# Loading the first weights in three transfers instead of four, and the sink rows of v partly copied on chip

## The chip, the cores and the metric

One core of one Trainium2 chip runs the kernel. The core has a matrix engine (PE; its weight loads are shown apart as PEld), a vector engine (DVE), an activation engine (ACT), a general engine (POOL) and a sequencer that only issues transfers and waits (SP). SP, ACT and POOL each issue DMA transfers, which the profile shows as queues: q1 is SP's, q10 ACT's and q0 POOL's. All queues share 16 DMA engines. The metric is the time of one execution on the device, in microseconds (us).

## The reference

Attention with a window and with sinks, followed by a gated two-layer network over all heads:

```python
batch, n_heads, seq, head_dim = 4, 8, 768, 64;  n_sink, window = 4, 128
scores = q @ k^T / sqrt(64)
keep = (key < 4) | ((0 <= query - key) & (query - key < 128))
a = softmax(where(keep, scores, -1e9))
x = (a @ v) with the heads side by side          # (3072, 512)
h = x @ w_in                                     # w_in  (512, 2048)
out = (h / (1 + exp(-beta * h))) @ w_out         # w_out (2048, 512), out (3072, 512)
```

All inputs and the output are float32 in device memory. The kernel computes in bfloat16 and sums in float32.

## The kernel before, in words

**Units and tiles.** Attention is cut into 32 units n: one batch, one pair of heads and one half (384 positions) of the sequence each. `place(n)` gives the batch (n // 8), the pair and the half. Four units make one token tile T of 384 tokens, and there are 8 token tiles. In the network a tile has 16 hidden blocks of 128 columns (the index i runs over all 128 of them, m = i mod 16 within the tile). A hidden block is four products of w_in with the tile's x (L814), a tanh on ACT (L822) and a gate on DVE (L835). Its contribution to the output is three products with w_out (L843), one for each 128 tokens.

**Attention.** For units 0 to 11, q and k come by SP into float32 staging (L522), are cast to bfloat16 by POOL (for q of the first four by DVE, L621), transposed on PE (L652, L634), and multiplied into scores (L700), on which ACT takes the exponential (L707). From unit 12 on, POOL's transfers cast on the way (`land`, L552) and a DMA transpose on SP turns them (L567). v is cast into `v_aug`: for the first units by POOL's engine from staging (`cast_v`, L532), later by casting transfers (`load_v`, L542; `land_v`, L561). The product with v (L770) also gives the softmax sums; DVE takes the reciprocal (`rden`, L779) and scales (L781).

**Sinks.** A unit of the second half also attends to the first four keys of its sequence. Their keys come through `k_rows` (L592) into `k_sink`. The four rows of v lie in `v_sink`: for head 0 of each pair in partitions 0 to 3 and for head 1 in partitions 32 to 35, for all 16 pairs of batch and heads. Before the change two POOL transfers (L596) of 64 rows of 64 elements each, one for each head, bring all of them from device memory. They are read by the product at L759, which opens the sums of a second-half unit; the first such unit is unit 4.

**Weights.** w_in comes in four transfers of four blocks each (`load_w_in(m, 4)`, L578) issued by POOL, 1 MB of float32 each, which are cast on the way to 512 KB; one row of such a transfer is 512 elements, 2 KB. w_out comes in eight transfers of two blocks (L583).

**The order.** The kernel first collects every operation as a node with what it reads and writes. A planner then walks through time with estimated durations and a model of the transfers' landings, and puts each engine's nodes in the order in which they could start; ties go to the earlier written. What comes out is a fixed order for each engine; on the chip each engine runs it in order and waits on semaphores. A changed landing in the planner's model can thus change the order of other work. While PE has nothing to do before the first hidden block, the planner puts in fill products of a tile of ones (L450); from the first hidden block on there are none.

**Around the change.** POOL's first instructions alternate casts and issues: the first w_in transfer after `cast_v(0)`, the sink keys, the second w_in transfer, `cast_v(2)`, the third (14.02 us), `cast_v(3)`, the fourth (15.57), then `k_sink` and the masks, the two sink transfers of v (20.92), three loads of v, and the transfers of w_out with casts of q and k of units 4 to 7 in between. SP's loads of q and k of units 4 to 7 wait for the second w_in transfer to land; those of units 8 to 11 each wait for one of the w_out transfers. The later transfers of w_out wait for the third w_in transfer (block 8). The loop over s writes one step for each hidden block of the rest; s is not a time, but a place in the written order.

Of the kernel before, what the change touches and what calls it, by code (L numbers as in the profile page):

```python
# [9 lines left out]
B, H, S, D = 4, 8, 768, 64  # L10
NSINK, WINDOW = 4, 128
# [14 lines left out]
HEAD1 = 32  # L26
# [29 lines left out]
AGENDA = {}  # L56
for n in range(4, 8):
    for step, at in (("in", n - 4), ("sink", 16), ("a", 16), ("b", 16), ("av", 17), ("out", 18)):
        AGENDA.setdefault(at if step == "in" else at + 1 * (n - 4), []).append((n, step))
# [297 lines left out]
def bass_streamingllm_window__then__act_swish_beta_kernel(  # L357
# [218 lines left out]
    def load_w_in(m, ms, after=()):  # L576
        here = slice(m * 128, (m + ms) * 128)
        op("gp", lambda e: e.dma_start(w_in16[:, :, here], w_in_src[:, :, here]), after=after,  # L578
           w=[("w_in", c, mm) for c in range(4) for mm in range(m, m + ms)],
           dma=f"wi{m}", late=0.0 if m else 800.0, **transfer(DM * ms * 128 * 4, 385, 740.0, 3.0))  # L580
# [3 lines left out]
           w=[("w_out", mm) for mm in range(m, m + ms)],  # L584
           dma=f"wo{m}", **transfer(ms * 128 * NOUT * 4, 416, 740.0, 3.0))

    def load_sinks(x, after=()):
        for hh in range(2):
            rows = slice(HEAD1 * hh, HEAD1 * hh + NSINK)
            if x:  # L590
                src = k[:, :, 0:NSINK, :].rearrange("b (g h) s d -> h (b g) s d", h=2)[hh]
                op("gp", lambda e, hh=hh, src=src: e.dma_start(k_rows[:, :, hh, :], src),  # L592
                   w=[("k_rows", hh)], after=after, dma=f"sk{hh}", busy=650.0, lag=300.0, weight=0.4)
            else:
                src = v[:, :, 0:NSINK, :].rearrange("b (g h) s d -> s h (b g) d", h=2)[:, hh]
                op("gp", lambda e, rows=rows, hh=hh, src=src: e.dma_start(v_sink[rows, :, hh, 0:D], src),  # L596
                   w=[("v_sink", hh)], r=["v_sink"], after=after, dma=f"sv{hh}", busy=650.0, lag=400.0, weight=0.4)

    def sink_keys():

# [144 lines left out]
    def attend(n, av_ps=av_ps, name="av"):  # L745
        _, hp, half, pb = place(n)
        z = n % NE
        where = {}
        x = 0
        for runs in RUNS[half]:  # L750
            for kb, qb, nq in runs:
                for y in range(nq):
                    where[kb, qb + y] = x
                    x += 1
        with P.together("pe"):
            for mm in range(3):
                m, at = 3 * half + mm, mm * 2 * D1
                if half == 1:
                    op("pe", lambda e, at=at, mm=mm: e.matmul(  # L759
                        av_ps[:, at:at + 2 * D1], E_sink[z][:, mm * 128:mm * 128 + 128],  # L760
                        v_sink[:, n // 8 * 4 + hp, :, :].rearrange("p h e -> p (h e)"),
                        start=True, stop=False, skip_group_check=True),
                       r=[("E_sink", z), "v_sink", ("v_sink", 0), ("v_sink", 1)], w=[name],
                       **pe(130))
                for hh in range(2):
                    kbs = range(m + 1) if half == 0 else (m - 1, m)
                    for x, kb in enumerate(kbs):
                        col = 128 * where[kb, m]
# [107 lines left out]
    load_w_in(0, 4, [("v", 0, 0, 0)])  # L876
    cast_v(1)
    cast(2)
    load_sinks(1, [("v", 1, 0, 0)])
# [15 lines left out]
    cast(3)  # L895
    load_w_in(4, 4, [("k16", 0)])
    cast_v(2)
    load_w_in(8, 4, [("v", 2, 0, 0)])
    cast_v(3)
    load_w_in(12, 4, [("v", 3, 0, 0)])  # L900
    for n in range(4):
        if n < 2:
            transpose_first(n + 2)
        if n < 3:
            first_scores(n + 1)
        if n == 2:
# [31 lines left out]
    for s in range(-2, S_END + NM):  # L938
# [102 lines left out]
```

## Time and profile before

| what | value |
|---|---|
| median of 3 runs | 228.73 us (228.01 to 229.79) |
| profiled execution | 228.59 us |
| its span, first to last instruction | 226.9 us |
| granted PE clock, mean | 1.000 |
| first hidden product | 17.32 us |
| first product with w_out | 35.08 us |
| first hidden product of the second token tile | 44.51 us |
| POOL issues | w_in 0.74 to 0.94 us, v_sink 0.65, load of v 0.90, land 0.76 |

The span is what the timeline covers; the profiled execution's own time is 1.7 us longer. In the timeline a row merges neighbouring instructions of the same kind: start, length, engine, line, operation, result and operands, count, and in brackets the engine's idle time before it with what ended it. The length of a row of products includes the time that the last one takes to come through the array, so that the next row may start before this one has ended. In the list of transfers, the time to landing is from the issue to the last semaphore update.

### The profile page before, as it was taken

Reading aid. Unit: us, or ns where it says so; the run is one execution under the profiler, and the core shown is the slowest. Engines: PE = TensorE matmul, PEld = TensorE weight load, DVE = VectorE, ACT = ScalarE, POOL = GpSimd, SP = SyncE. Lnnn points to the kernel's source line nnn. Section 1 sums busy time; section 2 is a strip of 40 time slices with the busy share of each in tenths; the row PEclk is TensorE's granted clock in tenths of the full one; section 3 lists DMA queues with packets and bytes.
Section 4 is the critical chain, followed back from the end, with each engine's and each line's share of the span. In section 5 each row is a group of like instructions: output and inputs, shape, how many; then the busy total and the mean of one; then the engine's idle time right before and its main releaser. Section 6 shows DMA issues by size and latency. Waiting matters only on the chain.

```text
span 226.9 us, 4463 instructions
## 1 busy us (share of the span) xinstructions
PE 220.0 (97%) x1761; PEld 122.1 (54%) x1761; DVE 132.6 (58%) x264; ACT 141.3 (62%) x224; POOL 125.7 (55%) x191
## 2 busy tenths in 40 slices
PE   7999989999999999999999999999999999999995
PEld 4665545555555555555555555555555555555454
DVE  5466777488975776566565656555656564443200
ACT  1877796197586877566657766666656755555311
POOL 4689992899994979695939396876300000000000
PEclk9999999999999999999999999999999999999999
DMA  6999999999998999999999999998921012110122
GB/s 172 251 172 179 276 194 205 257 228 139 118 138 124 124 117 151 120 167 144 116 113 135 99 138 147 96 165 119 94 80 53 20 57 64 49 46 0 58 83 92
DMA packets 96901, 28.92 MB, mean 127 GB/s; under 512 B 83424, under 2 KB 93936, under 8 KB 96880
## 3 DMA queue, kind: packets, MB, share of 16 engines
q0 software_dynamic: 59232, 10.92, 65.7%
q1 hardware_dynamic: 34304, 16.79, 34.3%
q10 hardware_dynamic: 3344, 0.93, 1.9%
q8 instruction: 14, 0.23, 0.5%
q14 instruction: 7, 0.06, 0.1%
HBM read 27.34 MB, written 6.29 MB: 148 GB/s over the span
## 4 chain that ended last, share of the span: by engine, by line
PE 73%; DMA 15%; POOL 8%; issue 2%; SPq 1%; ACT 0%; POOLq 0%; ACTq 0%
PE acc L843 32%; PE h_ps L814 29%; DMA k_stage<-in_k_dram 8%; DMA w_out<-in_moe_w_out_dram 4%; PE s_ps L727 4%; PE s_ps L770 4%; POOL qk L621 3%; DMA w_in<-in_moe_w_in_dram 2%; POOL land L552 2%; PE h_ps L843 2%; POOL v_aug L561 1%; PE s_ps L759 1%; PE s_ps L670 1%; SPq L522 1%; POOL v_aug L532 0%
## 5 line engine op out<-in xcount | busy, mean ns | idle before, releaser
L822 ACT ACTIVATE th<-h_ps,beta_half 128x384 f32<-128x384 f32 x120 | 69.4, 581 | 59.7 <-PE h_ps L814 59.1
L843 PE MATMUL acc<-w_out,g 128*128 128x512 bf16 x368 | 99.7, 380 | 0.0
L814 PE MATMUL h_ps<-xT,w_in 128*128 128x384 bf16 x480 | 96.2, 326 | 0.0
L835 DVE SCALAR_TENSOR_TENSOR g<-th,h_ps 128x384 bf16<-128x384 f32 x120 | 65.6, 550 | 44.8 <-ACT th L822 44.0
L814 PEld LDWEIGHTS h_ps<-xT,w_in 128*128 128x128 bf16 x480 | 45.6, 98 | 39.8 <-issue 0.8
L843 PEld LDWEIGHTS acc<-w_out,g 128*128 128x128 bf16 x368 | 32.8, 98 | 28.8 <-issue 3.6
L552 POOL DMA_DIRECT2D land<-in_q_dram x40 | 30.2, 760 | 24.0 <-DVE rden L779 24.0
L552 POOL DMA_DIRECT2D land<-in_k_dram x40 | 30.3, 761 | 0.0
L561 POOL DMA_DIRECT2D v_aug<-in_v_dram x40 | 30.2, 760 | 0.0
L735 ACT ACTIVATE E<-s_ps 128x1536 bf16<-128x1536 f32 x20 | 28.8, 1442 | 0.0
L741 DVE TENSOR_TENSOR E<-E,mask 128x1536 bf16<-128x1536 bf16 x20 | 19.2, 958 | 16.4 <-ACT E L735 16.4
L851 ACT ACTIVATE out_sb<-acc 128x512 f32<-128x512 f32 x23 | 13.7, 596 | 7.6 <-PE acc L843 7.4
L770 PEld LDWEIGHTS s_ps<-v_aug,E 128*128 128x128 bf16 x336 | 15.2, 97 | 3.2 <-issue 1.2
L770 PE MATMUL s_ps<-v_aug,E 128*128 128x65 bf16 x336 | 16.8, 193 | 0.0
L707 ACT ACTIVATE E<-s_ps 128x768 bf16<-128x768 f32 x17 | 13.7, 811 | 4.3 <-PE s_ps L700 4.2
L781 DVE TENSOR_TENSOR o_norm<-s_ps,rden 128x384 bf16<-128x384 f32 x28 | 15.6, 556 | 0.8
L714 DVE TENSOR_TENSOR E<-E,mask 128x768 bf16<-128x768 bf16 x16 | 9.0, 572 | 2.0 <-ACT E L707 1.3
L727 PE MATMUL s_ps<-qkT 64*128 64x256 bf16 (+2 forms) x144 | 10.1, 254 | 0.0
L759 PE MATMUL s_ps<-v_sink,E_sink 128*128 128x130 bf16 x48 | 9.3, 219 | 0.0
L621 POOL CAST qk<-k_stage 128x384 bf16<-128x384 f32 x12 | 6.5, 544 | 4.7 <-DMA k_stage<-in_k_dram 4.4
L673 ACT ACTIVATE E_sink<-s_ps 128x384 bf16<-128x384 f32 x16 | 7.8, 490 | 1.5 <-PE s_ps L670 1.5
L727 PEld LDWEIGHTS s_ps<-qkT 64*128 64x128 bf16 x144 | 4.9, 94 | 7.1 <-issue 5.8
(75 smaller groups left out, 155.2 us busy)
## 6 DMA issues: line engine op xcount, KB each, us to landing
out_dram<-out_sb SPq DMA_DIRECT2D x23, 256.0 KB, 2.7
q_stage<-in_q_dram SPq DMA_DIRECT2D x12, 192.0 KB, 7.4
k_stage<-in_k_dram SPq DMA_DIRECT2D x12, 192.0 KB, 7.9
w_in<-in_moe_w_in_dram POOLq DMA_DIRECT2D x4, 512.0 KB, 6.8
w_out<-in_moe_w_out_dram POOLq DMA_DIRECT2D x8, 256.0 KB, 9.6
land<-in_q_dram POOLq DMA_DIRECT2D x40, 48.0 KB, 3.7
land<-in_k_dram POOLq DMA_DIRECT2D x40, 48.0 KB, 4.0
v_aug<-in_v_dram POOLq DMA_DIRECT2D x40, 48.0 KB, 3.4
```

What stands on the lines that cost most here:

```text
L552: op("gp", lambda e, d=d, s=s: e.dma_start(d, s), w=[("land", pb, half, x, hh)], after=after, dma=f"l{pb}{half}{x}{hh}", **transfer(TT * D ...
L561: op("gp", lambda e, d=d, s=s: e.dma_start(d, s), w=[("v", pb, 3 * half + c, hh) for c in range(3)], after=after, dma=f"lv{pb}{half}{hh}", ...
L707: op("act", lambda e: e.activation(both, src[:, :, 0:TT], AF.Exp, bias=0.0, scale=SCALE), x=list(names), w=[("E", n % NE, c)], **act(768))
L727: op("pe", lambda e, at=at, w=w, kb=kb, qb=qb, nq=nq, hh=hh, rows=rows, bank=bank: e.matmul(s_ps[:, 2 * hh + bank, at:at + w], keys_of(pb, ...
L735: op("act", lambda e: e.activation(E[z][:, :, :], src, AF.Exp, bias=0.0, scale=SCALE), x=list(S_NAMES), w=[("E", z, 0), ("E", z, 1)], **ac ...
L741: op("dve", lambda e: e.tensor_tensor(E[z][:, :, :], E[z][:, :, :], m.unsqueeze(1).to_broadcast([128, 2, 768]), ALU.mult), r=[("E", z, 0), ...
L770: last=(x == len(kbs) - 1): e.matmul(av_ps[:, at + hh * D1:at + hh * D1 + D1], E[z][:, hh, col:col + 128], v_aug[:, pb, hh, kb, 0:D1], sta ...
L781: op("dve", lambda e: e.tensor_tensor(o_norm[o][:, :, :, :].rearrange("p m h d -> p (m h) d"), src[:, :, 0:D], rden[z][:, :].unsqueeze(2). ...
L814: op("pe", lambda e: e.matmul(bank, w_in16[:, c, m * 128:(m + 1) * 128], xT[:, c, T * TT:(T + 1) * TT], start=(c == 0), stop=(c == 3)), r= ...
L822: op("act", lambda e: e.activation(th[i % 3][:, :], bank, AF.Tanh, bias=0.0, scale=beta_half[:, m:m + 1]), x=[name], r=["beta"], w=[("th", ...
L835: op("dve", lambda e: e.scalar_tensor_tensor(g[T % 2][:, m, :], th[i % 3][:, :], 1.0, bank, ALU.add, ALU.mult), r=[("th", i % 3)], x=[name ...
L843: op("pe", lambda e: e.matmul(bank[:, 0:width], g[T % 2][:, m, t * 128:(t + 1) * 128], w_out16[:, m, cols], start=(m == 0), stop=(m == NM ...
```

## The change

- The third and the fourth transfer of w_in become one: `load_w_in(8, 8)` brings blocks 8 to 15, 2 MB of float32 in rows of 4 KB, where the third was issued. The fourth issue goes.
- The two early transfers of v's sink rows go. For batch 0, DVE copies them from `v_aug` (rows 0 to 3 of the first key block, which the casts have just written), one copy for each head, written where the transfers were. For batch 1, DVE copies them likewise, written at step 34 behind a reciprocal.
- For batches 2 and 3 two transfers each bring them, written at steps 48 and 80. The product at L759 now waits for its own batch's rows.
- `load_sinks` is split: the sink keys are loaded as before. `1 * (n - 4)` becomes `n - 4`, which is the same.

```diff
-    def load_sinks(x, after=()):
+    def load_sink_keys(after=()):
+        for hh in range(2):
+            src = k[:, :, 0:NSINK, :].rearrange("b (g h) s d -> h (b g) s d", h=2)[hh]
+            op("gp", lambda e, hh=hh, src=src: e.dma_start(k_rows[:, :, hh, :], src),
+               w=[("k_rows", hh)], after=after, dma=f"sk{hh}", busy=650.0, lag=300.0, weight=0.4)
+
+    def sink_values(b, eng, after=()):
         for hh in range(2):
             rows = slice(HEAD1 * hh, HEAD1 * hh + NSINK)
...
-                src = v[:, :, 0:NSINK, :].rearrange("b (g h) s d -> s h (b g) d", h=2)[:, hh]
-                op("gp", lambda e, rows=rows, hh=hh, src=src: e.dma_start(v_sink[rows, :, hh, 0:D], src),
-                   w=[("v_sink", hh)], r=["v_sink"], after=after, dma=f"sv{hh}", busy=650.0, lag=400.0, weight=0.4)
+            op(eng, lambda e, rows=rows, hh=hh: e.tensor_copy(
+                v_sink[rows, 4 * b:4 * b + 4, hh, 0:D], v_aug[0:NSINK, :, hh, 0, 0:D]),
+               r=["v_sink", *(("v", z, 0, hh) for z in range(4))], w=[("v_sink", b, hh)],
+               busy=200.0, lag=140.0, after=after)
+
+    def load_sink_values(b):
+        for hh in range(2):
+            rows = slice(HEAD1 * hh, HEAD1 * hh + NSINK)
+            src = v[b, :, 0:NSINK, :].rearrange("(g h) s d -> s h g d", h=2)[:, hh]
+            op("gp", lambda e, rows=rows, hh=hh, src=src: e.dma_start(
+                v_sink[rows, 4 * b:4 * b + 4, hh, 0:D], src),
+               w=[("v_sink", b, hh)], r=["v_sink"], after=[("rden", 0)], dma=f"sv{b}{hh}", busy=650.0, lag=400.0, weight=0.4)
...
-                       r=[("E_sink", z), "v_sink", ("v_sink", 0), ("v_sink", 1)], w=[name],
+                       r=[("E_sink", z), "v_sink", ("v_sink", n // 8, 0), ("v_sink", n // 8, 1)], w=[name],
...
-    load_w_in(8, 4, [("v", 2, 0, 0)])
+    load_w_in(8, 8, [("v", 2, 0, 0)])
     cast_v(3)
-    load_w_in(12, 4, [("v", 3, 0, 0)])
...
-            load_sinks(0, [("v", 3, 0, 0)])
+            sink_values(0, "dve")
...
+        if s == 34:
+            sink_values(1, "dve", [("rden", 1)])
+        if s in (48, 80):
+            load_sink_values(2 if s == 48 else 3)
```

More of the change, by code (lines that the diff above doesn't have):

```diff
@@ L58 @@
     for step, at in (("in", n - 4), ("sink", 16), ("a", 16), ("b", 16), ("av", 17), ("out", 18)):
-        AGENDA.setdefault(at if step == "in" else at + 1 * (n - 4), []).append((n, step))
+        AGENDA.setdefault(at if step == "in" else at + n - 4, []).append((n, step))
 for n in range(8, NU):
@@ L585, in load_w_out @@
            dma=f"wo{m}", **transfer(ms * 128 * NOUT * 4, 416, 740.0, 3.0))
-    def load_sinks(x, after=()):
+    def load_sink_keys(after=()):
[4 more added lines that the diff above has]
+    def sink_values(b, eng, after=()):
         for hh in range(2):
             rows = slice(HEAD1 * hh, HEAD1 * hh + NSINK)
[L590 to L594, printed above, removed]
-                src = v[:, :, 0:NSINK, :].rearrange("b (g h) s d -> s h (b g) d", h=2)[:, hh]
-                op("gp", lambda e, rows=rows, hh=hh, src=src: e.dma_start(v_sink[rows, :, hh, 0:D], src),
-                   w=[("v_sink", hh)], r=["v_sink"], after=after, dma=f"sv{hh}", busy=650.0, lag=400.0, weight=0.4)
+            op(eng, lambda e, rows=rows, hh=hh: e.tensor_copy(
[9 more added lines that the diff above has]
+               w=[("v_sink", b, hh)], r=["v_sink"], after=[("rden", 0)], dma=f"sv{b}{hh}", busy=650.0, lag=400.0, weight=0.4)
     def sink_keys():
@@ L878, in bass_streamingllm_window__then__act_swish_beta_kernel @@
     cast(2)
-    load_sinks(1, [("v", 1, 0, 0)])
+    load_sink_keys([("v", 1, 0, 0)])
     select(ident32[:, :], ones32[:, :], [[1, 32]], ALU.is_equal, 0.0, 0, -1, ["ones32"], ["ident32"])
```

## The prediction

> **What bounds the kernel now.** I read the page's first part, then the chain of waits, then the timeline of PE stretch by stretch, then the DMA queues in narrow windows.
>
> The page's first part, and the longer pieces of the chain before 62 us (start, length, what):
>
> ```profile
> PE 220.0 (97%) x1761; PEld 122.1 (54%) x1761; DVE 132.6 (58%) x264; ACT 141.3 (62%) x224; POOL 125.7 (55%) x191
> ...
> 12.45 5.50 DMA w_in<-in_moe_w_in_dram
> 18.37 7.79 DMA k_stage<-in_k_dram
> ...
> 27.81 9.58 DMA w_out<-in_moe_w_out_dram
> 37.82 7.45 DMA k_stage<-in_k_dram
> ...
> 58.58 0.53 POOL qk L621
> ```
>
> After 59 us the chain is PE alone, one product behind the other to the end. So only what lies before 62 us can move the time. There the chain goes from transfer to transfer, and PE waits in small pieces. Its timeline (start, length, what, idle time before):
>
> ```profile
> 21.91 1.46 PE L814 MATMUL acc<-xT,w_in 128*128 128x384 bf16 x8
> 23.21 1.46 PE L814 MATMUL h_ps<-xT,w_in 128*128 128x384 bf16 x8
> 24.51 1.76 PE L814 MATMUL acc<-xT,w_in 128*128 128x384 bf16 x8
> 26.15 0.34 PE L634 MATMUL s_ps<-ident,qk 128*128 128x128 bf16 x3
> 26.78 0.34 PE L634 MATMUL s_ps<-ident,qk 128*128 128x128 bf16 x3 [0.29 <-POOL qk L621]
> ...
> 30.49 0.60 PE L634 MATMUL s_ps<-ident,qk 128*128 128x128 bf16 x6 [0.42 <-ACT qkT L641]
> ...
> 31.58 0.34 PE L700 MATMUL h_ps<-qkT 64*128 64x128 bf16 x4 [0.22 <-ACT E L707]
> ...
> 34.81 0.34 PE L700 MATMUL h_ps<-qkT 64*128 64x128 bf16 x4 [0.36 <-ACT E L707]
> ...
> 59.16 0.34 PE L634 MATMUL s_ps<-ident,qk 128*128 128x128 bf16 x3 [0.47 <-POOL qk L621]
> ```
>
> Eight hidden products start 1.30 us apart (21.91, 23.21, 24.51), so one takes 0.1625 us, and a block of four 0.65. The shown length contains a drain, so real idle is larger than the bracket: between starts, less issue slots, I get 0.34 before 26.15, 0.46 before 26.78, 0.8 around 30, about 1.9 from 31 to 35, and 0.35 at 50.2 and 0.64 at 58.5, where PE waits for POOL's casts. That is some 4.5 us in all which a better start could remove at most.
>
> The DMA queues: first 25 to 27 us, then 29 to 31, then 36 to 38 (packets, MB written, share). q0 is POOL's queue, q1 is SP's.
>
> ```profile
> q1 hardware_dynamic: 784, 0.57, 94.8%
> q0 software_dynamic: 499, 0.02, 23.6%
> ...
> q0 software_dynamic: 2059, 0.27, 205.1%
> q1 hardware_dynamic: 113, 0.08, 16.5%
> ...
> q0 software_dynamic: 427, 0.41, 124.2%
> ```
>
> From 25 to 27 us POOL's queue moves 0.02 MB: exactly the two sink transfers (8 KB each), and nothing behind them. SP's loads of q and k have the engines meanwhile.
>
> **The change, part by part.**
>
> *The third and fourth MB of w_in in one transfer.* Issues and landings before, from the windows around each issue: third 14.02 + 7.9 = 21.9, fourth 15.57 + 9.8 = 25.4. Hidden block 8, the first that reads them, comes at 21.91 + 0.65 = 22.56: just behind the landing. Now blocks 8 to 15 all wait for the whole 2 MB. When does it land? It is issued where the third was. Late bound: 25.4, the same bytes behind the same queue, with the same eight loads of SP (released by the second MB, at 17.96) beside them. Early bound: the queue alone moves a w_out MB in 2.5 us (four landings 1.28 us apart), so 17.94 + 2 x 2.5 = 23.0. The case nearest to it is the fourth MB itself; with half the packets I take 25.2. PE then stands still for 25.2 - 22.56 = 2.6 us (0.5 to 2.9). Nothing else is ready for it: the fill products end with the first hidden block, and the next transposes need casts of loads that land at 25.2 and 26.2.
>
> The Trainium skill, DMA: Bandwidth & Descriptors, Anatomy of one DMA, has a fixed 2.0 us for each such transfer beside bytes / 436 GB/s; by that one issue of 2 MB in place of two would land about 2 us earlier and the stall would be some 0.6 us. The 1.28 us between landings of queued 512 KB transfers shows no fixed part, so here I don't count it.
>
> What of the 2.6 us comes back: blocks 8 to 15 now run 25.2 to 30.4 and, with 12 transposes of 0.055, to about 31. That work lies where PE idled before (0.34 + 0.46 + 0.8 = 1.6 us). PE is 1.0 us late at 31 (range -1.1 to +1.3). ACT gets its tanh later too (eight of 0.615 us after 25.2); it then has a solid chain of exponentials, 29.65 to 36.2 before.
>
> *One POOL issue less (0.74 us and 0.3 of wait), and the two sink loads less (1.29 us).* POOL comes 2.3 us earlier to the loads of v and w_out, but it waits anyway for casts whose data land at 25.2 and later, and idles 4.48 us before 38.97. Worth 0 by itself; what it buys is that the queue behind w_in is full earlier.
>
> *The two sink transfers out of POOL's queue.* Their own bytes are worth about 0.1 us, the whole stretch 2.0. In that stretch the engines worked for SP, so most of it isn't lost time: when v's rows come in earlier, SP's loads share sooner. By bytes read, 25 to 27 moved 0.61 MB and 27 to 29, mixed, 0.51, against 0.62 for 29 to 31; I count 0.5 us of throughput. w_out's first landing (24.85 + 10.0 = 34.9) comes at 33 to 34.3; the products that read it can fill part of the 1.9 us idle from 31 to 35. How many, the written order decides (bounds 0 and 1.9); I take 0.7. PE is then 1.0 - 0.7 = 0.3 late near 40.
>
> *The sink copies on DVE.* Four copies of 4 partitions; nearest rows: 72 ns for a memset of 4x16, 0.55 us for a 128x384 cast. The first two fall near 15.3 to 16, beside the normalisation of units 2 and 3, and may push the first hidden block by 0 to 0.6 us; the stall at block 8 covers that. If the stall weren't there, it would cost that much. The other two are written behind the eleventh block of the second token tile (tanh rows 45.4 to 58.6 are eleven), so near 59 us, where DVE is 90% busy (9.02 of 10 us) but PE waits for POOL: 0, at most 0.4.
>
> *The late sink loads.* Two POOL issues of 0.65 us at each of two places, and perhaps 2 us of POOL's queue, as at 25. Behind them wait the land transfers; their transposes land 6.7 us or more ahead of the scores that read them, mostly 12 to 19. Hidden: 0. Without that cover it would be 2 to 3 us.
>
> *From 45 to 62.* The chain w_out, SP's loads, POOL's casts comes at best 0.5 us earlier; POOL's own issues before the cast at 45.31 leave only its 0.42 us wait. PE late by 0.3 there eats part of the two waits of 1.0 us, so the end moves with POOL: -0.3 (bounds +1.3 and -2.9, all good ends or all bad ends together).
>
> **The sum.** -0.3 us on the profiled execution's 228.59 (span 226.9 and 1.7 around it): 228.3. The median of the three runs is 228.73, within their spread of 228.01 to 229.79.
>
> **Rivals.**
>
> *The early w_out fills every gap.* PE's 1.9 us up to 35 go, attention of units 4 to 7 ends earlier, POOL's land issues wait less for DVE (0.6 at 40.5) and its chain starts earlier. For: q0 stood still 2 us. Against: ACT is busy 5.00 of 5 us from 30 to 35, and the stall comes first. About -2: 226.5.
>
> *Units 4 to 7 become late (slower).* v's small packets now run from about 25 beside SP's loads. Between 27 and 29, so mixed, SP got 514 packets, against 784 from 25 to 27; k of units 5 to 7 land 1 to 1.5 us later (28.5, 30.1, 31.9 before). With the tanh work pushed into the same time, ACT reaches the end of its exponentials 1.5 to 2 us later; the normalisations that release POOL's land issues at 40.49 follow, and POOL's unbroken run from 45 to 59, on which PE waits at 58.5, with them. It decides once the lateness is above POOL's slack of 0.42: +1.3 to +2, 230.2. For: POOL's casts came within 0.3 us of those landings. Against: w_out products can fill PE.
>
> *PE's clock falls in the stall.* In the first microseconds PE runs at half speed: 13 fill products in 1.57 us, less one drain of 0.29, are 0.107 us apart; 7 at 16.59 in 0.55, less 0.22, 0.055. The rows at 5.83 and 7.14 show the change between them, so some 5.5 us slow. After that no idle piece is over 0.8 us, and the granted clock stays 1.0. An idle piece of 2.6 us is new; were the slow stretch to come again, 2.8 us: 231.1. The Trainium skill, TensorE: Matmul & The Clock Gate, What's actually happening, gives an idle window of about 3.4 us as what throttles; by that 2.6 us would not, a later landing could. No row of this trace has a pause so long.
>
> **How the numbers follow.** Forecast, with its own range 227.2 to 229.4: 0.62. Early fill, 226.5: 0.14. Late units, 230.2: 0.16. Clock, 231.1: 0.08. A range of 226.5 to 230.4 leaves out half of the first rival, a third of the second and nearly all of the third, 0.2. A measurement of this kernel tells about 1% from no change: under 226.4 faster, over 231.0 slower. Faster takes half of the early fill and a little tail, 0.09; slower takes half of the clock and a quarter of the late units with a tail, 0.10; the rest, 0.81, is the same.
>
> **What would show it.** A wait of PE's weight loads for w_in of 2 to 3 us at about 22.6; no 0.02 MB stretch in POOL's queue at 25; first product of w_out before 34.5; first hidden block of the second token tile (44.51 before) within 1 us of that; no wait for sinks or DVE copies. Wrong if PE has real idle after 62, if the w_in wait is below 1 us, or if the order puts so much else in front that PE reaches the second token tile over 1.5 us early or late.

## The result, and the profile after

The changed kernel takes 230.41 us (median of 22 executions, 229.12 to 232.93), the kernel before, run beside it on the same chips, 228.72 us. The ratio is 1.008, with a 95% interval of 1.0057 to 1.0103: a small but clear loss of 1.3 to 2.4 us. The forecast of 228.3 us had the wrong sign, and 230.41 lies just past 230.4, the end of its wide range, and a full 1 us past 229.4, the end of the range that it held likeliest. A ratio, here and below, leaves out single executions more than 1.5% above the fastest of their kernel; a median is of all.

The profiled execution after took 231.46 us with a span of 229.7 us, 2.9 us over that of before. It is not a typical one: it lies 1 us above its median. Before anything that the change touches, its first reciprocal (unit 0) comes at 13.31 us, 11.02 before. Two things lie ahead of that. Loads of q and k landed up to 0.9 us later (q of the second unit at 7.26, 6.34 before), and PE's clock was released later: its products are still 0.107 us apart, the spacing of the first microseconds, at 12.1 us, where before the last ones so far apart stand at 6.2. In the 17 profiles of this document the first reciprocal comes anywhere between 10.97 and 13.31 us. So absolute times after are read with some 2.3 us of this in mind, and the verdicts below rest on all executions of a kernel.

The page's first part, then the pieces of the chain of waits before 62 us that answer to those shown of before (start, length, what):

```profile
PE 219.5 (96%) x1734; PEld 122.8 (53%) x1761; DVE 134.3 (58%) x268; ACT 141.4 (62%) x224; POOL 126.8 (55%) x192
...
16.49 1.58 DVE v_sink L597
...
26.00 11.96 DMA w_out<-in_moe_w_out_dram
...
45.01 2.95 POOL land L552 x4
```

Work has not grown: PE has as many weight loads as before (1761). Its busy time cannot be compared, since 27 records of products are missing from this profile (1734 of 1761). Behind 62 us the chain is again PE, but for two pieces of 0.6 us, and from 92 us to the end every weight load of a hidden block starts 2.8 to 3.0 us later than before: nothing more is lost there. New in the chain is a copy of the sinks' rows at 16.49, which the forecast had covered by a stall, and POOL's four issues of `land` at 45.01, which began at 40.49 before. PE's timeline of the changed kernel (start, length, what, idle time before):

```profile
24.99 0.81 PE L825 MATMUL acc<-xT,w_in 128*128 128x384 bf16 x4
26.11 0.34 PE L645 MATMUL s_ps<-ident,qk 128*128 128x128 bf16 x3 [0.31 <-POOL qk L632]
26.29 0.81 PE L825 MATMUL acc<-xT,w_in 128*128 128x384 bf16 x4
...
35.74 0.59 PE L854 MATMUL acc<-w_out,g 128*128 128x512 bf16 x2 [0.99 <-DMA w_out<-in_moe_w_out_dram]
...
48.54 0.34 PE L645 MATMUL s_ps<-ident,qk 128*128 128x128 bf16 x3 [0.52 <-POOL qk L632]
48.72 0.98 PE L825 MATMUL h_ps<-xT,w_in 128*128 128x384 bf16 x5
```

There is no wait for w_in at all: the 2 MB landed at 25.29. What PE waits for after block 7 (24.99) is POOL's cast of unit 4. The products at 26.11 are the transposes of unit 4, and block 8 stands behind them at 26.29. Before, PE ran blocks 8 to 12 (22.56 to 26.1) and came to these transposes at 26.15. On the way it stood 0.28 us for the fourth MB of w_in, which landed at 25.40; PE's weight load of block 12, before:

```profile
25.44 0.44 PEld L814 LDWEIGHTS acc<-xT,w_in 128*128 128x128 bf16 x4 [0.50 <-DMA w_in<-in_moe_w_in_dram]
```

So the written order has changed around the transfer that was merged: with one landing for blocks 8 to 15 the planner takes them as later than unit 4's data. Everything behind follows late: the reciprocals of units 4 to 7 end at 38.1 to 45.76 (34.25 to 42.8 before), and the second token tile begins at 48.72 (44.51).

### The profile page after: what moved, and what is told of

The parts are those of the page before. It is cut to its first block, busy times and chain, and to the rows that moved or that the text cites. A ratio compares the mean times of both kernels' runs of the same rounds, so it can differ in the third digit from the quotient of the medians.

```text
span 229.7 us, 4447 instructions
## 1 busy us (share of the span) xinstructions
PE 219.5 (96%) x1734; PEld 122.8 (53%) x1761; DVE 134.3 (58%) x268; ACT 141.4 (62%) x224; POOL 126.8 (55%) x192
## 3 DMA queue, kind: packets, MB, share of 16 engines
q1 hardware_dynamic: 34304, 16.79, 33.7%
HBM read 27.32 MB, written 6.29 MB: 146 GB/s over the span
## 4 chain that ended last, share of the span: by engine, by line
PE 75%; DMA 10%; POOL 9%; DVE 2%; issue 1%; ACT 0%; SPq 0%; ACTq 0%; POOLq 0%
PE acc L854 31%; PE h_ps L825 29%; DMA w_out<-in_moe_w_out_dram 5%; DMA q_stage<-in_q_dram 5%; PE s_ps L781 4%; PE s_ps L738 4%; POOL land L552 4%; POOL qk L632 2%; PE h_ps L854 2%; POOL v_aug L561 1%; POOL v_aug L542 1%; PE s_ps L770 1%; PE s_ps L681 1%; DVE v_sink L597 1%; PE s_ps L663 1%
## 5 line engine op out<-in xcount | busy, mean ns | idle before, releaser
L854 PE MATMUL acc<-w_out,g 128*128 128x512 bf16 x341 | 94.5, 380 | 2.3 <-DMA w_out<-in_moe_w_out_dram 1.0
L561 POOL DMA_DIRECT2D v_aug<-in_v_dram x40 | 30.5, 766 | 0.0
L542 POOL DMA_DIRECT2D v_aug<-in_v_dram x6 | 5.3, 886 | 5.4 <-DMA w_out<-in_moe_w_out_dram 5.0
```

The lines of the kernel that those rows point to most:

```text
L561: op("gp", lambda e, d=d, s=s: e.dma_start(d, s), w=[("v", pb, 3 * half + c, hh) for c in range(3)], after=after, dma=f"lv{pb}{half}{hh}", ...
L854: op("pe", lambda e: e.matmul(bank[:, 0:width], g[T % 2][:, m, t * 128:(t + 1) * 128], w_out16[:, m, cols], start=(m == 0), stop=(m == NM ...
```

## The experiments

The theories that the expectations weigh against each other:

- **Copy**: DVE's copy of the sinks' rows, slow beside POOL's zeroing of `k_sink`, delays PE (in the first records, theory A).
- **POOL's order**: POOL's cast for unit 8 now stands ahead of its loads for unit 12, and these come late (B).
- **Landing**: blocks 8 to 15 wait for 2 MB together, and less of that comes back than forecast (C and D).
- **Order**: the new written order, with the transposes of unit 4 ahead of block 8, makes PE stand for POOL's cast whatever the weights do (E).

### Each part alone

The kernel before with only the merged transfer; its order is the planner's new one:

```diff
-    load_w_in(8, 4, [("v", 2, 0, 0)])
+    load_w_in(8, 8, [("v", 2, 0, 0)])
     cast_v(3)
-    load_w_in(12, 4, [("v", 3, 0, 0)])
```

> Only the third and fourth MB of w_in are put in one transfer; the sink rows of v come as before. Theory A, the copy beside the memset (the first sink copy on DVE took 1.66 us where its like took 0.21, while POOL's memset of k_sink ran, and it holds up the start of the network): nothing of the loss is here, 228.4 to 229.2 against 228.7 before. Theory B, the written order (with one landing for blocks 8 to 15 the planner puts the cast of q of unit 8 ahead of POOL's four land issues, and POOL's unbroken run from 45 us starts later): most of the loss is here, 229.7 to 230.5. Theory C, the forecast's stall: PE waits 1 to 3 us for w_in at block 8 and the time is up to 1 us longer.

And the changed kernel with w_in back in four transfers, so that only the sinks differ from before:

```diff
-    load_w_in(8, 8, [("v", 2, 0, 0)])
+    load_w_in(8, 4, [("v", 2, 0, 0)])
     cast_v(3)
+    load_w_in(12, 4, [("v", 3, 0, 0)])
```

> Only the sink rows of v are changed (copies on DVE for batches 0 and 1, late loads for 2 and 3); w_in in four transfers as before. Theory A: the first copy takes about 1.7 us beside POOL's memset, the first hidden product comes 1.5 to 1.9 us later, and the time is 1 to 1.7 us longer, 229.7 to 230.4. Theory B: the order keeps the land issues ahead of the cast of unit 8; no loss, 228.2 to 229.0. Theory C: no loss.

Measured: the merged transfer alone 231.52 us, ratio 1.0084 (1.0048 to 1.012), which is the whole loss; the sinks alone 228.79 us, 0.9992 (0.9963 to 1.0021), which is nothing. The late loads of the sinks are free, as the forecast had it, and the copies are free too when nothing slows them. Taking the two early transfers out of POOL's queue, on which the forecast set 0.7 us, shows no gain either, though the interval reaches down to 0.4%. Part of the merged transfer's loss comes with PE's clock: seven of its twelve executions have a mean granted clock of 0.993 or 0.985 and a median of 232.34 us, the five at full clock 230.13, 0.5% over before.

### The copy beside POOL's zeroing

The changed kernel with the zeroing of `k_sink` among the constants at the start:

```diff
+        fill("gp", k_sink[:, :, :], 0.0, ["k_sink"], busy=1800.0)     # in constants()
...
-            fill("gp", k_sink[:, :, :], 0.0, ["k_sink"], busy=1800.0, after=[("v", 3, 0, 0)])
```

> The changed kernel, with POOL's memset of k_sink written among the constants, so that it runs in POOL's idle time between 3 and 5 us and no longer beside DVE's first sink copy; the planned order of DVE and PE stays. Theory A: both first copies take 0.2 to 0.3 us, the first hidden product comes 1.5 us earlier than in the changed kernel for the same start, and the time is 228.6 to 229.2. Theory B: 229.9 to 230.5, as the changed kernel's 230.4, since the cast of unit 8 still stands ahead of the land issues.

Measured: 231.48 us, ratio 1.0107 (1.0067 to 1.0147); nothing is recovered. The run does not clear the copies, since against its expectation the planner rewrote the order of DVE, ACT and POOL here too, and PE stands 1.79 us for POOL's cast of unit 4 (from 24.50) and 1.91 us for that of unit 8 (from 47.53). But the collision itself is real. The copies up to 62 us in the changed kernel (shortest, median, longest in ns), and DVE's and POOL's timelines there:

```profile
L597 DVE COPY v_sink<-v_aug x4: 208/230/1660, 16.4 to 61.0; 4x256 bf16<-4x256 bf16 x4
...
16.19 1.81 POOL L444 MEMSET k_sink<- 128x2048 bf16 x1
...
16.41 1.91 DVE L597 COPY v_sink<-v_aug 4x256 bf16<-4x256 bf16 x2
```

The first copy takes 1660 ns, its like 208 to 236 ns, and it ends at 16.41 + 1.66 = 18.07 us, 0.07 behind the zeroing (16.19 + 1.81 = 18.00). With the zeroing early, the same copy took 215 ns. With w_in in four transfers it took 216 ns as well, because POOL's fourth issue holds the zeroing back to 17.43: taking that issue away is what put the two side by side. The Trainium skill, SBUF — State Buffer, SBUF: two separate sides, says that DVE in its two-port mode and POOL hold one pair of ports by an exclusive lock and that the later one is blocked until the other is done; the trace agrees in that the copy ends just behind the zeroing each time it falls in it (also 18.34 behind 18.27, in the run of section "Order and landing apart"). It does not show that the later one waits: in that run the copy's record starts at 16.44 and the zeroing's at 16.46, and in the first run of the next section at 16.04 and 16.06, and it is the copy that waits. Whether the copy runs in that mode no view shows.

### POOL's order

The changed kernel with POOL's loads for unit 12 held ahead of its casts for unit 8, as they stood before (operations with the same `seq` keep the order in which they are written):

```diff
-            op("gp", lambda e, d=d, s=s: e.dma_start(d, s), w=[("land", pb, half, x, hh)], after=after,
+            op("gp", lambda e, d=d, s=s: e.dma_start(d, s), w=[("land", pb, half, x, hh)], after=after, seq="p8" if n == 12 else None,
...
-               r=[(name + "_stage", pb, half)], w=[(name + "16", z)],
+               r=[(name + "_stage", pb, half)], w=[(name + "16", z)], seq="p8" if n == 8 else None,
```

> The changed kernel, with POOL's four land issues of unit 12 held ahead of the casts of unit 8 in POOL's order, as before the change. Theory A: 230 to 230.8, as the changed kernel, since the start of the network is late all the same. Theory B: POOL casts k of unit 8 near 46 us instead of 48, and the time is 228.6 to 229.4.

Measured: 230.32 us, 1.006 (1.0035 to 1.0084), no clear recovery. The opposite was tried too: POOL's casts for units 10 and 11 ahead of later loads, in the kernel before, and in the kernel with the sinks' part alone.

```diff
-    casts.update({FIRST[n] - 2: n for n in range(8, XBAR)})
+    casts.update({FIRST[n] - (2 if n < 11 else 4): n for n in range(8, XBAR)})
```

(and the same `seq` on the casts of units 8 to 11 and the loads of units 13 and 14)

> The kernel before, with POOL's casts of units 10 and 11 put ahead of the land issues of unit 14 (and the transfer of v for unit 13). In all profiles so far the last instruction ended 168.3 to 168.9 us behind POOL's cast of k of unit 11. If that cast, at the end of POOL's run, sets the end: it comes 3 to 4 us earlier, PE's two waits for POOL (0.35 and 0.64 us) go, and the time is 0.5 to 1.0 us shorter. If PE is the bound there, it stays within 0.3 us.

> The sinks' part of the change alone (w_in in four transfers), with the same casts put ahead. If POOL's run sets the end: 0.5 to 1.0 us shorter than the sinks' part alone (228.8), so 227.8 to 228.4 for a kernel before of 229. If not: as the sinks' part alone.

Measured: 228.47 us, 0.9989 (0.9967 to 1.001), and 229.27 us, 1.0017 (0.9987 to 1.0047). POOL's last cast for PE in this stretch came at 54.13 us in the first, 58.58 before, and the time stayed. So POOL's unbroken run from 45 to 59, on which the forecast hung the end, does not set it by itself.

### Order and landing apart

The program can be told to keep a given order on each engine. First, the merged transfer with exactly the order of before, and the other way round, four transfers with the order that the planner wrote for the merged one. The beginning of PE's order where the two part (before, then new):

```
before:  block 7, blocks 8 to 12, transposes of q and k of unit 4, blocks 13 to 15, ...
new:     block 7, transposes of q of unit 4, blocks 8, 9, transposes of k, blocks 10 to 12, ...
```

> Only the third and fourth MB of w_in in one transfer, and every engine's order kept as it was before the change (the fourth issue simply goes). Theory D, the landing: PE stands at hidden block 8 from about 22.6 us until the 2 MB land (23.9 to 25.4), tanh and exponentials of units 4 to 7 follow, the reciprocal of unit 6 comes near 42 instead of 40.2, POOL's land issues behind it, and the time is 0.8 to 1.8 us longer, 229.6 to 230.8 for a kernel before of 229. Theory E, the order: the wait for w_in is taken back in the idle pieces behind it, and the time is within 0.5 us of before.

> Four transfers of w_in as before the change, and every engine's order as the planner wrote it for the merged transfer (transposes of unit 4 ahead of block 8, the cast of unit 8 ahead of POOL's land issues). Theory D, the landing: w_in is there at 22 us, and the time is within 0.5 us of before. Theory E, the order: PE stands ahead of block 8 all the same, for the cast of unit 4's q at 25 to 26 us, the reciprocal of unit 6 comes at 42 or later, and the time is 0.8 to 2 us longer.

Measured: merged in the old order 229.48 us, 1.0042 (1.0014 to 1.007); four transfers in the new order 231.42 us, 1.0121 (1.0076 to 1.0165). PE's timeline in the first, then PE's weight loads in the second:

```profile
22.09 0.81 PE L814 MATMUL acc<-xT,w_in 128*128 128x384 bf16 x4
24.72 0.82 PE L814 MATMUL acc<-xT,w_in 128*128 128x384 bf16 x4 [1.82 <-DMA w_in<-in_moe_w_in_dram]
...
36.64 0.59 PE L843 MATMUL acc<-w_out,g 128*128 128x512 bf16 x2 [0.16 <-issue]
```

```profile
23.27 0.58 PEld L814 LDWEIGHTS acc<-xT,w_in 128*128 128x128 bf16 x4
26.17 0.17 PEld L634 LDWEIGHTS s_ps<-ident,qk 128*128 128x128 bf16 x3 [2.32 <-POOL qk L621]
```

The same hole of about 2 us ahead of block 8, from two causes. In the first it is the forecast's: block 8 waits for w_in (24.68). In the second the third MB had landed at 21.36, and PE stands for POOL's cast of unit 4. So the landing alone costs, and the order alone costs; in the merged kernel with its own order the two fall into each other.

How the two sizes compare is less sure than the medians look. The second run has a further hole, of 1.48 us from 17.67, for which the new order is to blame as well. ACT's copies into `k_sink`, which wait for POOL's zeroing of it, now stand ahead of ACT's last copy of xT, which the first hidden block reads; before, that copy ran first (16.79) and those at 18.15. ACT's timeline and PE's in the second run:

```profile
18.18 0.42 ACT L611 COPY k_sink<-s_ps 64x64 bf16<-64x64 bf16 x2 [2.10 <-POOL k_sink L444]
18.61 0.48 ACT L802 COPY xT<-s_ps 128x384 bf16<-128x384 bf16 x1
...
19.15 0.34 PE L814 MATMUL acc<-xT,w_in 128*128 128x384 bf16 x1 [1.32 <-ACT xT L802]
```

With w_in in four transfers the zeroing ends late (18.14), as POOL's fourth issue holds it back. In the merged transfer alone it ends at 17.20, and the hole is 0.36 us. So four transfers in the new order cost more than that order costs in the merged kernel. The clock adds to it: at full clock the merged transfer in the old order is 0.2% over before (nine of twelve executions), four transfers in the new order 0.5% (three of six).

The same two cells with the sinks' part in: the changed kernel in the order that the planner writes for four transfers (called the good order below: blocks 8 to 10, transposes of q of unit 4, blocks 11 and 12, transposes of k), and four transfers in the changed kernel's order.

> The whole changed kernel (one 2 MB transfer, sinks copied and loaded late), but with every engine's instructions in the order that the planner writes for the same sinks with w_in in four transfers: hidden blocks 8 to 13 ahead of the transposes of unit 4. Theory order (the transposes of unit 4 ahead of block 8 make units 4 to 7 late; the landing itself costs 0.2 to 0.5%): ratio 1.002 to 1.005, 229.2 to 229.9 us where before is 228.75; the idle piece ahead of block 8 waits for w_in; normalisation of unit 6 ends before 42.3, block 15's last product starts before 31. Theory landing (2 MB that land together are the whole cost, however the work is written): as the changed kernel, ratio 1.007 to 1.010, 230.4 to 231. Theory of the sinks' copy (1.7 us on DVE beside POOL's memset) adds to either 0 to 0.3%, as the idle piece ahead of block 8 covers it.

> Sinks as in the changed kernel, w_in in four transfers, and every engine's instructions in the order of the changed kernel (transposes of unit 4's q ahead of block 8). Theory order: ratio 1.006 to 1.012, 230.1 to 231.5 us where before is 228.75, although the third MB lands near 21.5; PE stands about 2 us ahead of unit 4's transposes, waiting for POOL's cast and not for w_in. Theory landing: with the third MB early again the loss is gone, ratio 0.998 to 1.002, 228.3 to 229.2 us.

Measured: 231.16 us, 1.010 (1.0066 to 1.0133), and 230.08 us, 1.007 (1.0042 to 1.0098). The order theory is borne out by the second, whose executions are at full clock but for one, and which differs from the sinks alone (0.9992) only in its order; PE stands 1.52 us there for the cast of unit 4, and 0.97 us for ACT's copy of xT. It is missed by the first, which was to be 1.002 to 1.005. In that first run the collision did harm. Its DVE timeline, and its windows of 1 us (PE's busy time and count, the granted clock, the DMA engines' share, GB/s):

```profile
16.44 2.15 DVE L597 COPY v_sink<-v_aug 4x256 bf16<-4x256 bf16 x2 [1.47 <-POOL v_aug L532]
...
17.00:18.00 1.00, 0.54 (x9) 1.00 1.23 205
18.00:19.00 1.00, 0.00 (x0) 1.00 1.06 138
19.00:20.00 1.00, 0.28 (x5) 1.00 1.07 197
20.00:21.00 1.00, 1.00 (x13) 0.54 1.12 190
21.00:22.00 1.00, 1.00 (x4) 0.50 1.09 201
22.00:23.00 1.00, 1.00 (x4) 0.50 1.12 200
23.00:24.00 1.00, 1.00 (x6) 0.75 1.03 201
```

PE stands from 17.5 to 19.7, and from 20 to 23.5 its clock is granted at half: hidden products 0.32 us apart instead of 0.1625. Block 8 then starts at 27.32, 2 us behind its weights (25.28). Nine of the twelve executions have a mean clock of 0.993, which is what one such stretch makes of the mean (half of 3.4 us in 230); their median is 231.73, that of the three at full clock 229.56.

So the copies alone were moved, in both orders, behind DVE's copies of xT and so behind the zeroing:

```
DVE:   o_norm of unit 1, [copies out of here], rden and o_norm of unit 2, xT, rden and o_norm of unit 3, xT, [to here]
```

> f3_after_split_order (the changed kernel in the order that has blocks 8 to 13 ahead of unit 4) with one thing moved: DVE's two early copies of the sinks' rows stand behind its copies of xT instead of ahead of the normalisation of unit 2, so behind POOL's zeroing of k_sink. Copy theory (beside the zeroing the copy takes 1.7 to 1.9 us, PE stands 2.2 us at 17.5, and its clock halves for 3.4 us behind it, which is what made f3 slow in 9 of 12 runs): copies of 0.21 to 0.24 us, no idle piece over 1 us at 17.5, at most 3 of 12 runs with a mean clock of 0.993, ratio 1.002 to 1.005, 229.2 to 229.9 us where before is 228.75. Landing theory (2 MB together cost 0.8 to 1% in any order, the copy is nothing): ratio 1.007 to 1.010, as f3.

> The changed kernel in its own order with the same one thing moved: DVE's two early copies behind its copies of xT. Order theory (unit 4's transposes ahead of block 8 make units 4 to 7 late, and a late start is eaten by the wait that this makes): the late start goes (first hidden product near 18.5 where it was 20.4), but PE then stands about 2 us before unit 4's transposes or block 8, and the ratio stays at 1.006 to 1.010, 230.1 to 231 us. Copy theory alone (the copy and the clock behind it are what the change costs): ratio 1.002 to 1.004, 229.2 to 229.7 us.

Measured: in the good order 230.17 us, 1.0065 (1.0032 to 1.0099); in the changed kernel's own order 230.78 us, 1.0075 (1.0048 to 1.0102). The copies took 230 to 319 ns, and the hole at 17.5 was gone. Two of twelve and five of twelve executions still had a mean clock of 0.993 or 0.985, and so had seven of twelve of the merged transfer alone, which has no such copies: other idle pieces seem to do it too. Neither run is told apart from its partner with the copies ahead, since the intervals overlap. In the good order the ten executions at full clock have a median of 229.78, 0.45% over before. PE's timeline there, and PE's weight loads in the other:

```profile
23.37 0.81 PE L825 MATMUL acc<-xT,w_in 128*128 128x384 bf16 x4
26.27 0.82 PE L825 MATMUL acc<-xT,w_in 128*128 128x384 bf16 x4 [2.09 <-DMA w_in<-in_moe_w_in_dram]
```

```profile
23.19 0.58 PEld L825 LDWEIGHTS acc<-xT,w_in 128*128 128x128 bf16 x4
25.66 0.17 PEld L645 LDWEIGHTS s_ps<-ident,qk 128*128 128x128 bf16 x3 [1.89 <-POOL qk L632]
```

In the second, the changed kernel without the late start, the hole in front of unit 4 is plain: w_in had landed at 24.76, the cast came at 25.66.

### The transposes alone

With w_in in four transfers, only unit 4's six transposes (and DVE's copy of them) were moved: out of the front in the changed kernel's order, and into the front in the good order.

```diff
 good order, then transposes forward (PE):
  block 7
+ transposes q4
  block 8
  block 9
+ transposes k4
  block 10
- transposes q4
  block 11
  block 12
- transposes k4
```

> f4_split_after_order (w_in in four transfers, the changed kernel's order, 1.007) with only unit 4 put back: its six transposes stand behind hidden blocks 10 and 12 instead of ahead of block 8 and behind block 9, and DVE's copy of them behind the gate of block 11; ACT, POOL and SP as in f4. Theory transposes (PE standing in front of unit 4's cast is the price of the order): no idle piece over 1 us at 24, block 8 near 23.5, ratio 0.998 to 1.002, 228.3 to 229.2 us where before is 228.75. Theory rest of the order (the later mixing of attention and network products, or POOL's cast ahead of the loads of unit 12): stays at 1.005 to 1.009.

> e2_sinks_only (w_in in four transfers, sinks as in the changed kernel, 0.999) with only unit 4's six transposes put forward: ahead of hidden block 8 and behind block 9, and DVE's copy of them behind the gate of block 8; ACT, POOL and SP as in e2. Theory transposes: PE stands 1.5 to 2.2 us ahead of block 8 waiting for POOL's cast, part comes back behind it, ratio 1.004 to 1.010, 229.7 to 231 us. Theory rest of the order: stays within 0.3% of before.

Measured: transposes back 230.94 us, 1.0088 (1.0059 to 1.0117); transposes forward 231.45 us, 1.0115 (1.0081 to 1.0149). Forward, they alone cost what the whole new order costs, without the hole for ACT's copy of xT, and with PE standing from 22.96 for the cast (four of the six executions have a mean clock of 0.992 or 0.993; the two at full clock are 0.5% over before):

```profile
22.31 0.81 PE L825 MATMUL acc<-xT,w_in 128*128 128x384 bf16 x4
24.98 0.34 PE L645 MATMUL s_ps<-ident,qk 128*128 128x128 bf16 x3 [1.85 <-POOL qk L632]
```

Backward they did not bring the time back, against the expectation. The hole only moved: PE's timeline there has

```profile
27.65 0.33 PE L645 MATMUL s_ps<-ident,qk 128*128 128x128 bf16 x3
29.35 0.51 PE L645 MATMUL s_ps<-ident,qk 128*128 128x128 bf16 x6 [1.38 <-DVE qkT L652]
```

where unit 5's transposes now stand directly behind unit 4's and wait for DVE's copy of them. The hole of 0.98 us for ACT's copy of xT, which the order of this run still has, stayed too (from 18.32). So that run does not clear the rest of the order; it shows two other holes.

### A search for something better

The kernel before with POOL's casts ahead, as above, and the zeroing of `k_sink` at the start.

> The kernel before, with POOL's casts for units 10 and 11 written ahead of its land issues of unit 14, and with the zeroing of k_sink (1.8 us of POOL) among the constants at the start. A search for a version better than both. Theory order: POOL reaches the casts of units 4 to 7 up to 1.8 us earlier, but these wait for their data (25.2 us and later) anyway, so little is to be had: ratio 0.995 to 1.000, 227.6 to 228.7 us. If POOL's run from 45 to 59 set the end, it would be 0.99 or less, 226.5 us.

Measured: 229.74 us, 1.0046 (1.0026 to 1.0067), slower. The planner rewrote the order here too: the first transposes of unit 4 stand ahead of block 10, and PE waits 0.78 us for the cast. Whether that is the whole price was not tried. No run beat the kernel before by more than the measurement can tell.

### All runs together

PE time lost between 15 and 30 us in each profile, worked out as the gaps between the starts of successive products, less what a product of that width takes in a row (0.1625 us for 384 columns, 0.055 for 128), pieces over 0.06 us, each counted whole where it begins; half clock counts as loss. The last column gives the executions with a mean granted clock of 0.999 or 1.000, and their median over that of before at the same clock:

| run | w_in | order around block 8 | PE lost, 15 to 30 us | ratio | at full clock |
|---|---|---|---|---|---|
| casts ahead | 4 | as before | 0.98 | 0.999 | 10 of 12: 0.999 |
| sinks and casts ahead | 4 | as before | 1.32 | 1.002 | 10 of 12: 1.001 |
| sinks only | 4 | as before | 1.35 | 0.999 | 11 of 12: 0.999 |
| before | 4 | | 2.02 | 1 |  |
| casts ahead, zeroing early | 4 | unit 4 ahead of block 10 | 2.37 | 1.005 | 11 of 12: 1.005 |
| merged, old order | 3 | as before | 2.44 | 1.004 | 9 of 12: 1.002 |
| changed kernel | 3 | unit 4 ahead | 2.50 | 1.008 | 13 of 22: 1.007 (of all of before) |
| changed, copies behind | 3 | unit 4 ahead | 2.79 | 1.008 | 7 of 12: 1.005 |
| merged alone | 3 | unit 4 ahead | 2.92 | 1.008 | 5 of 12: 1.005 |
| changed, zeroing early | 3 | unit 4 ahead | 2.93 | 1.011 | 7 of 7: 1.010 |
| changed, good order, copies behind | 3 | as before | 3.00 | 1.007 | 10 of 12: 1.004 |
| transposes forward | 4 | unit 4 ahead | 3.32 | 1.012 | 2 of 6: 1.005 |
| four transfers, changed order | 4 | unit 4 ahead | 3.42 | 1.007 | 11 of 12: 1.006 |
| transposes back | 4 | hole at 27.8 | 3.49 | 1.009 | 6 of 6: 1.009 |
| four transfers, new order | 4 | unit 4 ahead | 4.04 | 1.012 | 3 of 6: 1.005 |
| changed, good order | 3 | as before | 4.30 | 1.010 | 3 of 12: 1.004 |
| changed, loads of unit 12 first | 3 | unit 4 ahead | 4.41 | 1.006 | 4 of 12: 1.004 |

The four kernels without a larger loss than before are the four that are not slower; all thirteen with more are, by 0.4 to 1.2%. Within the thirteen the loss in one profile does not rank the times: it is one execution, and a late start is partly eaten by the waits behind it. At full clock the thirteen are still 0.2 to 1.0% slower, so the holes cost by themselves; the halved clock, which comes in some executions of most runs with such a hole, adds to that. It is one reason why four transfers in the new order and the transposes forward look dearer than the rest.

## Why the prediction was wrong, step by step

**(1) The stall at block 8** was of the right kind and size in the order that the forecast assumed: 25.2 us for the landing, 24.68 in the run that keeps the order and start of before; 2.6 us of standing, 1.98 there and 2.25 in the changed kernel with the good order and the copies behind. Its return was nearly right as well, as far as 30 us: in the merged kernel with the old order block 8 starts 2.2 us late, and block 15's last product 1.37 us (30.11 against 28.74), 1.0 forecast. One row was misread on the way: most of the 0.34 us put ahead of 26.15 lies at 25.16 and is a wait for w_in, whose fourth MB came 0.28 us too late for block 12 already before the change.

**(2) The step that failed first is what the forecast set against it**: 0.7 us of idle time filled by earlier products of w_out, which was to leave PE 0.3 us late near 40. The two sink transfers did leave POOL's queue, but the queue hardly gained. The changed kernel from 25 to 27 us (packets, MB written, share):

```profile
q1 hardware_dynamic: 760, 0.55, 95.5%
q0 software_dynamic: 340, 0.04, 32.9%
```

0.04 MB instead of 0.02: v's small rows now stand where the sinks' rows stood, beside the same loads of SP. In this late execution the first landing of w_out came at 35.46 (34.88 before, 33 to 34.3 forecast), and its first product at 35.74 (35.08). Where the start is less late, in the changed kernel with the copies behind, they came at 34.14 and 34.19, within the forecast; yet its second token tile begins 2.9 us late behind a start 1.4 us late, 1.5 us more where the forecast had 0.3. With the old order the first product came at 36.64, 2 us behind its landing (34.63), since attention is written ahead of it, and the second token tile began 1.33 us late (45.84 against 44.51): as late as block 15 had been, with nothing filled. In the changed kernel with the good order and the copies behind it is the same, 36.73 for a landing at 35.21. Of the 1.33 us, 0.7 came back only behind that, on the way to 62 us, and PE ends 0.6 us late. Hence +0.7 us in the medians where the sum had -0.3.

**(3) The order was not in the sum at all.** "Nothing else is ready for it" took the order of before as given. The merged landing changes the planner's times, and unit 4's transposes went ahead of block 8. That PE then stands for a cast is shown with the weights landed 4.8 us ahead of it (21.36 and 26.17; ratio 1.0121, part of it the hole for ACT's copy of xT), and with the transposes alone put forward (1.0115). The last sentence of the forecast named this as what would make it wrong, at over 1.5 us; it was 4.2 us at the second token tile, 2.3 of them there from the late first reciprocal of that one execution.

**(4) The sink copies** were priced at 0 to 0.6 us; in the changed kernel they took 1.9. The rows nearest to a copy held it between them (0.07 and 0.55 us; 0.22 measured), and what slowed the first, POOL's zeroing of `k_sink`, stood in the trace of before at 16.30, but POOL's missing issue had not been carried on to where it puts that zeroing. The cover did hold: with the copies out of the way the changed kernel's ratio stays at 1.0075.

**(5) POOL 2.3 us earlier worth nothing, the late sink loads hidden**: right, by the sinks alone (0.9992). Two issues for the sinks at 83.58 take 1.22 us, and no product waits for them.

**(6) The end moves with POOL's run from 45 to 59**: not borne out. Taking 4.4 us off the place of POOL's last cast moved the time by no more than 0.3%.

**The rivals.** The slower one, units 4 to 7 late, came true as far as POOL's `land` issues, and its price is near (230.2, measured 230.41): reciprocals 3.0 to 3.9 us late (2.3 to 3.2 with the copies behind, in an execution that starts earlier), POOL's `land` issues at 44.96 instead of 40.49. How that reaches the end, by POOL's run from 45 to 59, is what (6) does not bear out, so the agreement in price is partly luck. Its stated reason did not come true: k of units 5 and 6 landed at 28.10 and 29.98 (28.46 and 30.13 before), so no transfer of SP was late; only unit 7's was, 33.35 for 31.87. What made the units late was PE's own order, the landing, and in the profiled execution its late start. The clock rival happens, in part of the executions, and costs about 2 us where nothing behind absorbs it (231.73 against 229.56; in the merged transfer alone 232.34 against 230.13). It does not carry the changed kernel's loss: its 13 executions at full clock have a median of 230.34, the other nine 230.58. In the merged transfer alone, in seven of twelve executions, it is a good part of the loss. The gain from an early fill by w_out never came.

What stays open: how much of the new order's price lies in unit 4's transposes, in ACT's copy of xT and in its later part, since taking the transposes back made another hole and left that copy where it was; how the landing and the order share the loss in the merged kernel; and what decides whether PE's clock halves behind an idle piece of 2 us in a given execution.

## What to carry to other kernels

When a planner writes the order, a change of one transfer is a change of every engine's order, and the sum must be made on the new order or say what it costs if the order moves. Merging two transfers takes the earlier landing away from the first half of the data; here blocks 8 to 11 were read as they landed, and the saved issue and the 4 KB rows bought at most some 0.4 us of landing in return, for data that were wanted 2 us earlier. An instruction taken off one engine moves all that stands behind it on that engine, and what it then falls beside on another is part of the price.

## What the runs showed of the hardware

- A DVE copy of 4 partitions by 256 elements takes 0.21 to 0.24 us in most places (up to 0.53 in some), and 1.66 to 1.90 us in the three profiles in which it falls into POOL's zeroing of 128x2048 elements (1.81 us); it ends 0.07 us behind the zeroing.
- In two profiles an idle piece of PE of about 2.2 us (17.5 to 19.7, 17.2 to 19.3) was followed by some 3.4 us at half the clock. Nine and eight of twelve executions of these two kernels have a mean clock that fits one such stretch; in a kernel with an idle piece of 2.25 us at 24 instead, two of twelve. The Trainium skill, TensorE: Matmul & The Clock Gate, What's actually happening, gives an idle window of about 3.4 us for it; these pieces are shorter.
- Rows of 4 KB hardly hastened the weights: from the landing of the second MB to that of the last of w_in it is 5.7 to 7.1 us in the eight profiles with one transfer of 2 MB (median 6.4), 5.7 to 8.7 in the nine with two transfers (median 6.8).
